# Operand addresses at a multiple of 64, differences on GpSimd alone, eight places for the x forms, and other ends, in a fused attention and two feed-forward layers

## The chip, the cores and the metric

The kernel runs on one core of a Trainium2 chip. The metric is the device time of one execution in microseconds (us); lower is better. TensorE (PE) multiplies matrices out of SBUF into PSUM, and the profile shows its weight loads apart (PEld). VectorE (DVE) and ScalarE (ACT) read PSUM and SBUF, GpSimd (POOL) works on SBUF tiles alone here, and SyncE (SP) issues every DMA.

## The reference, cut to what matters

```python
def _attn_ref(q, k, v):                       # (4, 8, 576, 64), block-causal mask
    scores = scale * np.matmul(q, k.transpose(0, 1, 3, 2))
    scores = np.where(mask, scores, -1000000000.0)
    attn = softmax(scores)
    return np.matmul(attn, v)
def _moe_ref(x, w_in, w_out):                 # x: 2304 x 512, w_in: 512 x 2048, w_out: 2048 x 512
    h = x @ w_in
    return (h * np.clip(h + 3.0, 0.0, 6.0) / 6.0) @ w_out
def _moe2_ref(x, w_in, w_out):                # the same sizes
    h = x @ w_in
    return (h * np.tanh(softplus(h))) @ w_out
# reference: attention, then _moe_ref on its output, then _moe2_ref on that
```

## The kernel before, in words

The program has three stages in a row. The **attention** fills the first 200 us. The **first layer** (to 618.8 us) goes through five blocks of tokens, four of 512 and one of 256, and in each through 16 slices `f` of the hidden width. A slice takes 12 matmuls in (L385 to L387) and 12 out (L851 to L853). Every product of two float32 operands is made of three matmuls in the type float32r: high part by high part, high by low, low by high. So each tile has a rounded tile (`wh`, `xh`, `gh`) and a rest (`wl`, `xl`, `gl`).

The **second layer** (618.8 to 998.8 us) multiplies by a scheme of seven products in place of eight (P1 to P7). Tokens go in three passes of 768, two halves of `NX` = 384 columns each; the hidden width goes in `NQ` = 8 steps `s` a pass, so there are 24 steps. A step has seven products "in" of 6 matmuls and seven "out" of 6, 84 matmuls of 384 columns in all, which `products` writes (L1150, L1152, L1153). Between in and out, ScalarE copies or activates (L1213), VectorE adds a PSUM bank to a kept tile (L1218), and then come differences of SBUF tiles: four sums T1 to T4 (`add_gsum`, L1229), and for each of the seven forms a rounding on ScalarE (L1222) and a rest, the tile less its rounding (`add_form`, L1224). VectorE adds every result of "out" to a running sum (L1199; L1197 at a pass's first step). The out products of step `s` run among the in products of step `s + 1`. The 11 differences of a step may go to VectorE or to GpSimd (`either`).

For each pass the tokens' own forms must be made too: four loads (`load2`, L985), eight differences (`sum2`, L994), 14 roundings (`round_x`, L1002) and 14 rests (`lower_x`, L1005). Form `i` of each pass lies in the same place `i`, so form `i` of the next pass can be written only when the last step of this pass has multiplied by it.

The order of the second layer is made at build time by `Schedule`: each operation has the engines that may run it with a cost in ns (`COST`), what it reads and writes, and for a DMA the time that it is taken to need to land (`land`). TensorE's order is as written. From it each other operation has a due time (`need`), and a list scheduler lets each engine take, of what is ready, the one that is due first. Each engine then runs its own list strictly in order: an operation whose input is late holds up what stands behind it. In the list, the loads of the next pass's tokens (`add_x`) come at the first step of a pass.

**Addresses.** In the program before, the weights of slices `f` = 0 to 3 lie at SBUF addresses of a multiple of 64 bytes, those of `f` = 4 to 15 (pool `whigh`, on the right side of SBUF) 32 bytes past one. The second layer puts its weights (`ws`) in the tiles of `f` = 7 to 14, all 32 past, and the x forms in those of `f` = 0 to 6. The tiles that the matmuls stream (`xh`, `xl`, `gh`, `gl`, and `gcP`) lie at a multiple of 64, but x forms 4 to 6 and the attention's `p`, `t` and `vh` 32 past one. The attention's `kb` and `qb` lie at a multiple of 64.

Of the kernel before, what the change touches and what calls it, by code (L numbers as in the profile page):

```python
# [9 lines left out]
F32 = mybir.dt.float32  # L10
# [95 lines left out]

NX = 384
# [6 lines left out]
    "in": 1040, "out": 520, "DVE_PSUM": 500, "DVE_SBUF": 800, "POOL": 1020, "ACT_PSUM": 490,  # L114
    "ACT": 530, "SP": 60,
# [3 lines left out]
class Schedule:  # L119
# [24 lines left out]
    def order(self):  # L144
# [72 lines left out]
def fused_kernel(ctx: ExitStack, tc: tile.TileContext, qT, kT, vv, w1, w2, outT):  # L217
# [9 lines left out]
    WLOW, WMID = 2, 4  # L227

# [772 lines left out]
    def round_x(i, k):  # L1001
        nc.scalar.activation(xc[FORMS[i], 0][:, k], xs2[FORMS[i], k], AF.Copy)  # L1002

    def lower_x(i, k, e="DVE"):
        ENG[e].tensor_sub(xc[FORMS[i], 1][:, k], xs2[FORMS[i], k], f32(xc[FORMS[i], 0][:, k]))  # L1005

    def prepare_x(i):
        place_x(i)
        for k in range(2):
            round_x(i, k)  # L1010
            lower_x(i, k, ("DVE", "POOL")[k])
# [109 lines left out]
    place_w(1, 1)  # L1121
    tile_of = lambda name: m5.tile([P, NX], F32, tag=name, name=name)
# [22 lines left out]
    either = (("DVE", COST["DVE_SBUF"]), ("POOL", COST["POOL"]))  # L1145

# [16 lines left out]
    def add_in(s, form):  # L1163
# [3 lines left out]
        def run(e):  # L1167
            products(
                bank[b], [weights_of(0, s, form, k) for k in range(2)],
                [(xc[form, 0][:, k], xc[form, 1][:, k]) for k in range(2)], new)  # L1170

        reads = w_names(0, s, form) + [("x", form, h, k) for h in range(2) for k in range(2)]
# [47 lines left out]
    def add_form(form):  # L1220
# [3 lines left out]
        plan.add(either, [src, ("g", form, 0)], [("g", form, 1)], lambda e: ENG[e].tensor_sub(  # L1224
            gc[form, 1], keep[src], f32(gc[form, 0])))

    def add_gsum(t):
        a, b = GSUM[t]
        plan.add(either, [a, b], [t], lambda e: ENG[e].tensor_sub(keep[t], keep[a], keep[b]))  # L1229
# [19 lines left out]
    def add_x_form(i):  # L1249
        form = FORMS[i]  # L1250
        for k in range(2):
# [3 lines left out]
            plan.add(act(False), [src], [("x", form, 0, k)], lambda e, k=k: round_x(i, k))  # L1255
            plan.add(either, [src, ("x", form, 0, k)], [("x", form, 1, k)],
                     lambda e, k=k: lower_x(i, k, e))
# [3 lines left out]
    for s in range(NS + 1):  # L1261
        q = s % NQ
        if s < NS and q == 0 and s // NQ + 1 < NPASS:
            add_x(s // NQ + 1)
        for i in range(7):
            if s < NS:
                form = IN_ORDER[i]
                b = add_in(s, form)
                if i in (3, 6):
                    add_weights(0, s + 2, i // 6)  # L1270
            if s:
                for d in range(2):
                    add_out(s - 1, OUT_ORDER[i], d)
                if i in (5, 6):
                    add_weights(1, s + 1, i - 5)
            if s == NS:
                continue
            if q == NQ - 1 and s + 1 < NS:
                add_x_form(i)
# [6 lines left out]
            elif form == "P2":  # L1286
                add_sum("g11", b, "p1")
                add_act("g11", "g11", AF.Mish, False)
                add_form("P1")
            elif form == "P3":  # L1290
                add_sum("g12", b, "g12")
                add_act("g12", "g12", AF.Mish, False)
                add_gsum("T1")
                add_form("P5")
            elif form == "P7":
                add_sum("g22", b, "g22")
                add_act("g22", "g22", AF.Mish, False)
                for t, g in (("T2", "P6"), ("T3", "P7")):
                    add_gsum(t)
                    add_form(g)  # L1300
                add_form("P3")
            else:
                add_act("g21", b, AF.Mish, True)
                add_form("P2")
                add_gsum("T4")
                add_form("P4")
# [43 lines left out]
```

## Time and profile before

| | us |
|---|---|
| median of 3 runs | 1005.14 (1003.14 to 1006.38) |
| the profiled execution, its own time | 1004.65 |
| its span, first to last instruction | 1002.7 |
| mean granted TensorE clock | 0.995 |

The profile is that of one execution. Its views: the busy time of each engine; what each engine waited for (in total, times, longest); the timeline, instruction by instruction, with the idle time before one and what ended it. Where the starts of two instructions are given, their difference is the time of what lies between. A matmul's own duration overlaps that of its neighbours, so its pace is read from starts.

### The profile page before, as it was taken

To read this page: it belongs to the slowest core of one execution; us is meant where nothing else is said; L and a number is where in the kernel's file an instruction comes from. 1 tells how busy PE (TensorE), PEld (TensorE's weight loads), DVE (VectorE), ACT (ScalarE), POOL (GpSimd) and SP (SyncE) were. 2 spreads that over 40 slices of the span, in tenths; PEclk is the share of its full clock that TensorE was granted. 3 is DMA by queue.
4 is the path that set the end of the run, shared out by engine and by line. 5 is a ranking of instruction groups with operands and counts; after the bars stand their busy time and mean duration, and the time that the engine had idled before them with its cause. 6 is when DMAs were issued, how large, how long until landed. Compare 5 with 4: busy or idle time off the path is not lost.

```text
span 1002.7 us, 15929 instructions
## 1 busy us (share of the span) xinstructions
PE 959.8 (96%) x5300; PEld 862.1 (86%) x5300; DVE 743.9 (74%) x1227; ACT 520.5 (52%) x1222; POOL 589.4 (59%) x548
## 2 busy tenths in 40 slices
PE   8999999899999998999999999799998999999997
PEld 7888889777778876888788899799998999999997
DVE  6898887888866454764647431789898898998887
ACT  4888888856534334343534353444464444654452
POOL 6455654568966656666667561645396453953453
PEclk9999999999999999999999999799999999999999
DMA  5777767789036664776665528567688676796652
GB/s 161 193 196 201 201 177 195 210 298 337 1 126 219 211 212 158 252 237 202 208 212 179 182 74 302 197 247 250 226 307 275 251 258 213 248 323 220 252 209 75
DMA packets 131425, 212.86 MB, mean 212 GB/s; under 512 B 45840, under 2 KB 72464, under 8 KB 131344
## 3 DMA queue, kind: packets, MB, share of 16 engines
q1 hardware_dynamic: 131344, 211.86, 64.9%
q8 instruction: 41, 0.67, 0.3%
q14 instruction: 40, 0.33, 0.1%
HBM read 154.66 MB, written 48.31 MB: 202 GB/s over the span
## 4 chain that ended last, share of the span: by engine, by line
PE 42%; POOL 4%; DVE 3%; DMA 2%; issue 2%; ACT 0%; SPq 0%; POOLq 0%; DVEq 0%
PE by L1150 5%; PE by L1153 5%; PE by L1152 5%; PE bh L1150 3%; PE bh L1152 3%; PE bh L1153 3%; PE y L852 2%; PE y L853 2%; PE y L851 2%; PE br L1153 2%; PE br L1150 2%; PE br L1152 2%; PE h L386 2%; PE h L387 2%; PE h L385 2%; DMA x2r<-x2d 2%
## 5 line engine op out<-in xcount | busy, mean ns | idle before, releaser
L1199 DVE TENSOR_TENSOR s<-by,s 128x384 f32<-128x384 f32 x306 | 160.0, 550 | 21.7 <-PE by L1153 21.7
L420 POOL TENSOR_TENSOR gl<-e,gh 128x512 fp32r<-128x512 f32 (+1 forms) x79 | 101.0, 1279 | 114.5 <-issue 66.1
L1229 POOL TENSOR_TENSOR kT<-kg,kg 128x384 f32<-128x384 f32 x44 | 46.3, 1053 | 160.2 <-ACT kg L1213 159.6
L385 PE MATMUL h<-xh,wh 128*128 128x512 f32 (+1 forms) x320 | 119.9, 375 | 5.0 <-DVE e L405 5.0
L1150 PE MATMUL by<-gcP,ws 128*128 128x384 f32 x336 | 115.8, 345 | 7.8 <-issue 5.7
L386 PE MATMUL h<-xl,wh 128*128 128x512 f32 (+1 forms) x320 | 119.2, 373 | 1.9 <-DVE xl L370 1.9
L852 PE MATMUL y<-gl,wh 128*128 128x512 f32 (+1 forms) x320 | 119.3, 373 | 1.8 <-POOL gl L420 1.8
L853 PE MATMUL y<-gh,wl 128*128 128x512 f32 (+1 forms) x320 | 119.0, 372 | 0.0
L851 PE MATMUL y<-gh,wh 128*128 128x512 f32 (+1 forms) x320 | 119.0, 372 | 0.0
L387 PE MATMUL h<-xh,wl 128*128 128x512 f32 (+1 forms) x320 | 118.9, 372 | 0.0
L1152 PE MATMUL by<-gcP,ws 128*128 128x384 f32 x336 | 113.7, 338 | 0.0
L1153 PE MATMUL by<-gcP,ws 128*128 128x384 f32 x336 | 113.7, 338 | 0.0
L412 ACT ACTIVATE gh<-e 128x512 fp32r<-128x512 f32 (+1 forms) x80 | 47.0, 587 | 121.1 <-DVE e L405 121.1
L1213 ACT ACTIVATE kg<-kg 128x384 f32<-128x384 f32 x72 | 37.8, 526 | 111.5 <-DVE kg L1218 111.5
L665 DVE TENSOR_TENSOR t<-t,t 128x512 fp32r<-128x512 f32 (+2 forms) x144 | 69.8, 521 | 23.5 <-ACT t L660 23.5
L282 DVE SCALAR_TENSOR_TENSOR v<-raw,v 128x512 uint32<-128x512 uint32 x64 | 70.8, 1119 | 20.1 <-POOL v L268 20.1
L394 ACT ACTIVATE e<-h 128x512 f32<-128x512 f32 (+1 forms) x80 | 43.9, 549 | 76.3 <-PE h L387 74.7
L614 ACT ACTIVATE p<-s,nm 128x64 f32<-128x64 f32 (+2 forms) x144 | 75.1, 529 | 11.9 <-DVE nm L603 11.9
L405 DVE SCALAR_TENSOR_TENSOR e<-e,h 128x512 f32<-128x512 f32 (+1 forms) x80 | 50.2, 628 | 40.5 <-ACT e L394 40.5
L1150 PE MATMUL bh<-xc,ws 128*128 128x384 f32 x192 | 65.9, 343 | 10.8 <-DVE kg L1218 10.6
L1150 PEld LDWEIGHTS by<-gcP,ws 128*128 128x128 f32 x336 | 63.4, 189 | 14.8 <-ACT gcP L1222 14.6
L385 PEld LDWEIGHTS h<-xh,wh 128*128 128x128 f32 x320 | 60.2, 188 | 18.1 <-DVE e L405 7.1
(116 smaller groups left out, 2675.5 us busy)
## 6 DMA issues: line engine op xcount, KB each, us to landing
ws<-w2d SPq DMA_DIRECT2D x96, 512.0 KB
ws<-w2d SPq DMA_DIRECT2D x96, 384.0 KB
raw<-w SPq DMA_DIRECT2D x64, 512.0 KB
x1d<-x SPq DMA_DIRECT2D x64, 144.0 KB
qb<-qs SPq DMA_DIRECT2D x30, 288.0 KB
w2d<-Sh SPq DMA_DIRECT2D x32, 256.0 KB
w2d<-S SPq DMA_DIRECT2D x32, 256.0 KB
q<-qT SPq DMA_DIRECT2D x16, 288.0 KB
```

Of the source, the lines that this page charges most:

```text
L385: nc.tensor.matmul(h, hi[:, ws], xh, start=(k == 0), stop=False)
L386: nc.tensor.matmul(h, hi[:, ws], xl, start=False, stop=False)
L387: nc.tensor.matmul(h, lo[:, ws], xh, start=False, stop=(k == KT - 1))
L420: eng.tensor_sub(gl, g, f32(gh))
L614: nc.scalar.activation(t, sc, AF.Exp, bias=nm[:, c:c + 1], accum_out=su[:, i:i + 1])
L851: nc.tensor.matmul(y, hi[:, ws], gh, start=first, stop=False)
L852: nc.tensor.matmul(y, hi[:, ws], gl, start=False, stop=False)
L853: nc.tensor.matmul(y, lo[:, ws], gh, start=False, stop=last)
L1150: nc.tensor.matmul(b, wh, xh, start=start and k == 0, stop=False, skip_group_check=True)
L1152: nc.tensor.matmul(b, wh, xl, start=False, stop=False, skip_group_check=True)
L1153: nc.tensor.matmul(b, wl, xh, start=False, stop=k == n - 1, skip_group_check=True)
L1199: nc.vector.tensor_add(dst, bank[b], total)
```

## The change

- A tile of 96 bytes a partition is put first on the right side of SBUF. All that lies there moves by 96 bytes, and what lay 32 past a multiple of 64 lies at one.
- The x forms have eight places in place of seven: form `i` of pass `p` lies in place `(i - p) % 8`. The eighth place is the tile of `f` = 15. So form `i` of the next pass goes where form `i - 1` of this pass lay.
- In steps `q` = 1 to 6 of each pass the 11 differences may go to GpSimd alone (`pool_`); in steps 0 and 7 to either engine, as before.
- The order of TensorE at the start and the end: P4 of step 0 comes after P1 of step 1; the in products of step 23 come two at a time between the out products of step 22.
- The roundings and differences of a step are added to the list after the out product of the step before; the loads of the next pass's tokens come at step `q` = 2, not 0.
- The scheduler's numbers: costs of VectorE and GpSimd are higher, `land` is 8000 for weights and 12000 for tokens (both 4000 before), and VectorE may wait for a more urgent operation that becomes ready while a less urgent one would run (`soon`).

No instruction is added or removed; the numbers of matmuls, DMAs and differences stay. The diff, cut:

```diff
+ALIGN = 96
-    "in": 1040, "out": 520, "DVE_PSUM": 500, "DVE_SBUF": 800, "POOL": 1020, "ACT_PSUM": 490,
-    "ACT": 530, "SP": 60,
+    "in": 1040, "out": 520, "DVE_PSUM": 550, "DVE_SBUF": 1200, "POOL": 1100, "ACT_PSUM": 490,
+    "ACT": 525, "SP": 60,
...
+                soon = [k for k in c if start < ready[k] < start + cost and need[k] < need[i]
+                        and need[k] < start + cost - self.HAND]
+                if soon and e == "DVE":
+                    i = min(soon, key=lambda i: (need[i], i))
+                    start, cost = ready[i], dict(ops[i][0])[e]
...
+    align = ctx.enter_context(tc.tile_pool(name="align", bufs=1, side="right"))
+    align.tile([P, ALIGN // 4], F32, tag="align", name="align")
...
-            t = slot(i, h, f"xc{i}_{h}")
-            xc[FORMS[i], h] = t[:, 0:2 * NX].rearrange("p (k n) -> p k n", k=2)
+            t = slot(i if i < 7 else 15, h, f"xc{i}_{h}")
+            xc[i, h] = t[:, 0:2 * NX].rearrange("p (k n) -> p k n", k=2)
+    def at_x(p, i):
+        return (i - p) % 8
...
+    place_x(7)
...
+    pool_ = (("POOL", COST["POOL"]),)
...
-                    lambda e, h=h: load_w(c, s, piece, h), land=4000)
+                    lambda e, h=h: load_w(c, s, piece, h), land=8000)
-                     lambda e, k=k: load2(p, k), land=4000)
+                     lambda e, k=k: load2(p, k), land=12000)
...
+    def sequence():
+        seq = []
+        for s in range(NS + 1):
+            for i in range(7):
+                if s == 1 and i == 0:
+                    seq += [("in", 1, 0), ("in", 0, 6), ("forms", 0, 6)]
+                elif 0 < s < NS - 1 or s == 0 and i < 6:
+                    seq.append(("in", s, i))
+                elif s == NS - 1 and i < 4:
+                    seq += [("in", s, n) for n in (2 * i, 2 * i + 1) if n < 7]
+                if s:
+                    seq.append(("out", s - 1, i))
+                if 0 < s < NS - 1 or s == 0 and i < 6:
+                    seq.append(("forms", s, i))
+                elif s == NS - 1:
+                    seq += [("forms", s, n) for n in {1: (3,), 2: (4,), 4: (5,), 6: (6,)}.get(i, ())]
+        return seq
...
-    for s in range(NS + 1):
-        q = s % NQ
-        if s < NS and q == 0 and s // NQ + 1 < NPASS:
-            add_x(s // NQ + 1)
+    for kind, s, i in sequence():
+        q, p = s % NQ, s // NQ
+        of = either if q in (0, NQ - 1) else pool_
...
+            if (q, i) == (2, 0) and p + 1 < NPASS:
+                add_x(p + 1)
```

## Rows read from the trace of the kernel before

**Rows 1.** The page: busy us (share of the span) xinstructions of each engine.
```profile
PE 959.8 (96%) x5300; PEld 862.1 (86%) x5300; DVE 743.9 (74%) x1227; ACT 520.5 (52%) x1222; POOL 589.4 (59%) x548
```
**Rows 2.** Timeline (start us, us, ...): first and last matmul of the second layer.
```profile
618.84 0.34 PE L1150 MATMUL bh<-xc,ws 128*128 128x384 f32 x1
...
998.51 0.34 PE L1153 MATMUL by<-gcP,ws 128*128 128x384 f32 x1
```
**Rows 3.** Timeline, one step of the second layer; then the next step's same matmul.
```profile
666.05 1.37 DVE L1224 TENSOR_TENSOR gcP<-kg,gcP 128x384 fp32r<-128x384 f32 x1
...
667.35 1.01 DVE L1199 TENSOR_TENSOR s<-by,s 128x384 f32<-128x384 f32 x2
667.35 0.34 PE L1153 MATMUL bh<-xc,ws 128*128 128x384 f32 x1
...
667.99 0.42 PE L1150 MATMUL by<-gcP,ws 128*128 128x384 f32 x1 [0.30 <-issue]
...
669.12 0.34 PE L1150 MATMUL br<-xc,ws 128*128 128x384 f32 x1
...
675.36 0.34 PE L1150 MATMUL br<-xc,ws 128*128 128x384 f32 x1
...
682.55 0.34 PE L1153 MATMUL bh<-xc,ws 128*128 128x384 f32 x1
```
**Rows 4.** Waits of the second layer: who for whom, us in total, times, longest.
```profile
PE by L1150 <- issue: 5.7, 19, 0.4
```
**Rows 5.** Timeline, start of the second layer.
```profile
624.91 0.34 PE L1153 MATMUL bh<-xc,ws 128*128 128x384 f32 x1
628.82 0.56 DVE L994 TENSOR_TENSOR x2t<-x2r 128x384 f32<-128x384 f32 x1 [9.36 <-DMA x2r<-x2d]
...
632.90 0.69 PE L1150 MATMUL bh<-xc,ws 128*128 128x384 f32 x1 [7.65 <-DVE kg L1218]
...
638.18 0.40 PE L1152 MATMUL by<-gcP,ws 128*128 128x384 f32 x1
```
**Rows 6.** Windows: us, each engine's busy us, PEclk (granted share of 2.4 GHz), DMA, GB/s.
```profile
634.00:636.00 2.00, 2.00 (x8) 2.00 (x8) 2.00 (x2) 1.03 (x3) 2.00 (x3) 0.50 0.05 9
```
**Rows 7.** Timeline, first step of the second pass.
```profile
758.90 0.45 PE L1150 MATMUL bh<-xc,ws 128*128 128x384 f32 x1 [2.92 <-DVE kg L1218]
```
**Rows 8.** Timeline, the last out products.
```profile
991.12 0.41 PE L1150 MATMUL by<-gcP,ws 128*128 128x384 f32 x1 [1.42 <-ACT gcP L1222]
```
**Rows 9.** Timeline, TensorE, first layer: bounds of 60 matmuls (`f` 1 to 3), of 240 (`f` 6 to 15).
```profile
301.84 0.40 PE L385 MATMUL h<-xh,wh 128*128 128x512 f32 x1
...
315.45 0.39 PE L385 MATMUL h<-xh,wh 128*128 128x512 f32 x1
...
420.87 0.39 PE L385 MATMUL h<-xh,wh 128*128 128x512 f32 x1
...
477.09 0.40 PE L385 MATMUL h<-xh,wh 128*128 128x512 f32 x1
```
**Rows 10.** The same in its block of 256 tokens: 48 matmuls (`f` 0 to 3); start of 264 (`f` 6 on).
```profile
575.94 0.28 PE L385 MATMUL h<-xh,wh 128*128 128x256 f32 x1
...
581.68 0.28 PE L385 MATMUL h<-xh,wh 128*128 128x256 f32 x1
...
587.86 0.28 PE L385 MATMUL h<-xh,wh 128*128 128x256 f32 x1
```
**Rows 11.** Timeline, attention: the first and third of three matmuls of 384 columns in a row.
```profile
49.31 0.34 PE L581 MATMUL s<-kb,qb 128*128 128x384 f32 x1
...
49.66 0.34 PE L583 MATMUL s<-kb,qb 128*128 128x384 f32 x1
```
**Rows 12.** Timeline, VectorE and GpSimd: a difference beside VectorE's, and one beside its adds.
```profile
682.17 1.31 POOL L1224 TENSOR_TENSOR gcP<-kT,gcP 128x384 fp32r<-128x384 f32 x1
...
992.72 4.73 DVE L1199 TENSOR_TENSOR s<-by,s 128x384 f32<-128x384 f32 x10
...
993.63 1.01 POOL L1224 TENSOR_TENSOR gcP<-kT,gcP 128x384 fp32r<-128x384 f32 x1
```

More of the change, by code (lines that the diff above doesn't have):

```diff
@@ L997, in place_x, with round_x, lower_x @@
         for h in range(2):
-            t = slot(i, h, f"xc{i}_{h}")
-            xc[FORMS[i], h] = t[:, 0:2 * NX].rearrange("p (k n) -> p k n", k=2)
[L1001 to L1005, printed above, removed]
+            t = slot(i if i < 7 else 15, h, f"xc{i}_{h}")
+            xc[i, h] = t[:, 0:2 * NX].rearrange("p (k n) -> p k n", k=2)
+    def at_x(p, i):
+        return (i - p) % 8
+    def round_x(p, i, k):
+        nc.scalar.activation(xc[at_x(p, i), 0][:, k], xs2[FORMS[i], k], AF.Copy)
+    def lower_x(p, i, k, e="DVE"):
+        hi, lo = (xc[at_x(p, i), h][:, k] for h in range(2))
+        ENG[e].tensor_sub(lo, xs2[FORMS[i], k], f32(hi))
     def prepare_x(i):
@@ L1009, in prepare_x @@
         for k in range(2):
-            round_x(i, k)
-            lower_x(i, k, ("DVE", "POOL")[k])
+            round_x(0, i, k)
+            lower_x(0, i, k, ("DVE", "POOL")[k])
     WSLOTS = {(0, 0): (7, 8), (1, 0): (9, 10), (0, 1): (11, 12), (1, 1): (13, 14)}
@@ L1169, in run @@
                 bank[b], [weights_of(0, s, form, k) for k in range(2)],
-                [(xc[form, 0][:, k], xc[form, 1][:, k]) for k in range(2)], new)
-        reads = w_names(0, s, form) + [("x", form, h, k) for h in range(2) for k in range(2)]
+                [(xc[at, 0][:, k], xc[at, 1][:, k]) for k in range(2)], new)
+        at = at_x(s // NQ, FORMS.index(form))
+        reads = w_names(0, s, form) + [("x", at, h, k) for h in range(2) for k in range(2)]
         plan.add(pe(COST["in"]), reads, [b], run)
@@ L1218, in add_sum, with add_form @@
             lambda e: nc.vector.tensor_add(keep[dst], bank[b], keep[other]))
-    def add_form(form):
+    def add_form(form, of):
         src = GFORM[form]
@@ L1223, in add_form, with add_gsum @@
             gc[form, 0], keep[src], AF.Copy))
-        plan.add(either, [src, ("g", form, 0)], [("g", form, 1)], lambda e: ENG[e].tensor_sub(
+        plan.add(of, [src, ("g", form, 0)], [("g", form, 1)], lambda e: ENG[e].tensor_sub(
             gc[form, 1], keep[src], f32(gc[form, 0])))
-    def add_gsum(t):
+    def add_gsum(t, of):
         a, b = GSUM[t]
-        plan.add(either, [a, b], [t], lambda e: ENG[e].tensor_sub(keep[t], keep[a], keep[b]))
+        plan.add(of, [a, b], [t], lambda e: ENG[e].tensor_sub(keep[t], keep[a], keep[b]))
     def add_weights(c, s, piece):
@@ L1247, in add_x, with add_x_form @@
                 plan.add(either, [at(a), at(b)], [at(out)], lambda e, k=k, n=n: sum2(k, n, e))
-    def add_x_form(i):
-        form = FORMS[i]
+    def add_x_form(p, i):
+        form, at = FORMS[i], at_x(p, i)
         for k in range(2):
@@ L1254, in add_x_form @@
                 "P6": ("T2", k), "P7": ("xB", k, 1), "P4": ("T4", k)}[form]
-            plan.add(act(False), [src], [("x", form, 0, k)], lambda e, k=k: round_x(i, k))
-            plan.add(either, [src, ("x", form, 0, k)], [("x", form, 1, k)],
-                     lambda e, k=k: lower_x(i, k, e))
+            plan.add(act(False), [src], [("x", at, 0, k)], lambda e, k=k: round_x(p, i, k))
+            plan.add(either, [src, ("x", at, 0, k)], [("x", at, 1, k)],
+                     lambda e, k=k: lower_x(p, i, k, e))
@@ L1259, in fused_kernel @@
     for piece in range(2):
         add_weights(1, 1, piece)
-    for s in range(NS + 1):
-        q = s % NQ
-        if s < NS and q == 0 and s // NQ + 1 < NPASS:
-            add_x(s // NQ + 1)
[L1265 to L1277, printed above, removed]
+    for kind, s, i in sequence():
+        q, p = s % NQ, s // NQ
+        of = either if q in (0, NQ - 1) else pool_
+        form = IN_ORDER[i]
+        if kind == "out":
+            for d in range(2):
+                add_out(s, OUT_ORDER[i], d)
+            if i in (5, 6):
+                add_weights(1, s + 2, i - 5)
+        elif kind == "in":
+            if (q, i) == (2, 0) and p + 1 < NPASS:
+                add_x(p + 1)
+            b = add_in(s, form)
+            if i in (3, 6):
+                add_weights(0, s + 2, i // 6)
@@ L1278, in fused_kernel @@
             if q == NQ - 1 and s + 1 < NS:
-                add_x_form(i)
+                add_x_form(p + 1, i)
             if form == "P1":
@@ L1288, in fused_kernel @@
                 add_act("g11", "g11", AF.Mish, False)
-                add_form("P1")
             elif form == "P3":
@@ L1292, in fused_kernel @@
                 add_act("g12", "g12", AF.Mish, False)
-                add_gsum("T1")
-                add_form("P5")
             elif form == "P7":
@@ L1297, in fused_kernel @@
                 add_act("g22", "g22", AF.Mish, False)
[L1298 to L1301, printed above, removed]
             else:
                 add_act("g21", b, AF.Mish, True)
-                add_form("P2")
-                add_gsum("T4")
-                add_form("P4")
+        elif form == "P2":
+            add_form("P1", of)
+        elif form == "P3":
+            add_gsum("T1", of)
+            add_form("P5", of)
+        elif form == "P7":
+            for t, g in (("T2", "P6"), ("T3", "P7")):
+                add_gsum(t, of)
+                add_form(g, of)
+            add_form("P3", of)
+        elif form == "P4":
+            add_form("P2", of)
+            add_gsum("T4", of)
+            add_form("P4", of)
     plan.issue()
```

## The prediction

> **What bounds the kernel now.** I read the busy times first: TensorE is busy 96% of the span [rows 1], so time is to be had only where it waits or where each matmul takes longer than it must. Then I took the pace of matmuls from starts on the timeline, stage by stage, and then the gaps.
>
> In the second layer, 36 matmuls of 384 columns run from 669.12 to 675.36 us without a gap, 173.3 ns each [rows 3]. The stage has 2016 matmuls, 2015 start-to-start intervals from 618.84 to 998.51 us, 379.67 us [rows 2]. At 173.3 ns they would take 349.2. So 30.5 us are lost there. They are in four kinds of place:
> - The start. After P7 of step 0 TensorE stands from 624.91 to 632.90, 7.99 us for an interval of 0.17. P4 waits until VectorE has read the bank of P7, and VectorE sits for 9.36 us in front of a token sum (L994) whose load has not landed. Then 16 intervals take 5.28 us (to 638.18), 330 ns each, where 2.77 would do: the granted clock in that stretch is 0.50, the 1.2 GHz level, after TensorE stood. Lost: 7.82 + 2.51 = 10.3 us [rows 5, 6].
> - The head of nearly every step. VectorE is on a difference of 1.37 us from 666.05, so the add that frees the bank of P1 starts at 667.35; TensorE goes from 667.35 to 667.99 between two matmuls and stretches the next. That is 0.47 + 0.08 = 0.55 us [rows 3]. The waits list has it 19 times [rows 4]: 10.5 us.
> - The second pass's first step, the same pattern: the add on VectorE that P4 needs comes late, behind token sums, and TensorE idles 2.92 us [rows 7]; with the slow matmul behind it 3.0.
> - The last out products: 1.42 us of waiting for a form [rows 8]; with the slow start 1.5.
>
> These are 25.3 of the 30.5; 5.2 are left in smaller waits and in matmuls a few ns over the floor.
>
> In the first layer, matmuls of 512 columns differ by their weights' address: 60 in `f` = 1 to 3 (a multiple of 64) take 13.61 us, 226.8 ns each; 240 in `f` = 6 to 15 (32 past) take 56.22 us, 234.2 ns each [rows 9]. What they stream is at a multiple of 64 in both.
>
> **The change part by part.** *Addresses, 512 columns.* 1152 matmuls of the first layer (12 slices x 24 x 4 blocks) have weights 32 past. At 7.4 ns each that is 8.5 us, if every one sets the pace. *256 columns.* Here it goes the other way: 48 at a multiple of 64 take 5.74 us, 119.6 ns; 264 at 32 past take 30.98 us (587.86 to 618.84 [rows 2, 10]), 117.3 ns. 288 matmuls x 2.3 ns cost 0.7. Net at most 7.8 us. I don't take it all: in the first block the weights' conversion on the other engines sets some of the pace, and stalls at the block boundaries wait for loads that don't get faster. I take 5.5, ends 2 and 7.8.
>
> *384 columns.* In the second layer almost all is 32 past in weights, and still 173.3 ns is reached. The attention's `kb` and `qb` are at a multiple of 64, and there two intervals take 0.35 us, 175 each [rows 11]. So I expect no new floor, only fewer of the odd longer ones: out of the 5.2 us left over I take 1.0, ends -2 (a loss as at 256 columns would be 2016 x 1 ns) and 3. *Attention.* `p`, `t` and `vh` move too. The trace shows no run of these at another address; nearest are [rows 9], a gain of 3%, and [rows 10], a loss of 2%; 448 matmuls of `t` by `vh` at no more than the 234 ns of 512 columns are under 105 us, so the bound is a gain of 3.2 to a loss of 2.1. I take 0.
>
> The Trainium skill's page "SBUF — State Buffer", section "Door 1: The DMA port swizzle", says that SBUF is read in lines of 16 bytes. Both 0 and 32 past a multiple of 64 begin such a line, so by that rule alone the move would change nothing; the trace disagrees at 512 columns, by 7.4 ns [rows 9], and what the rule would give is the first rival below.
>
> *Differences on GpSimd alone in steps 1 to 6.* VectorE's remaining work is 14 adds from "out" and 3 others, 17 x about 0.5 (ten back to back take 4.73 us [rows 12]), 8.5 us of a step of 84 x 173.3 ns = 14.56. It is then free when a bank ends. GpSimd does 11 differences. One takes 1.01 us where VectorE runs only adds from PSUM beside it, and 1.31 where VectorE has a difference as well [rows 12]. Eleven at 1.01 are 11.1 us, at 1.31 14.4: both below 14.56. Counting from a step's start, the longest chain begins when P7 ends at 11.4 us: add and activation to 12.7, T2 to about 14.6, rounding, the rest of P6 to about 16.7, needed at 19.8 when the next step's out P6 comes. Three us are spare, and the last one, P4's rest, ends near 22.7 against 28.1. So GpSimd's longer queue is hidden under TensorE; were the cover gone, each 0.1 us an operation would cost 1.1 us a step. Behind GpSimd's list stand only differences, and ScalarE's roundings wait for them; its own copies from PSUM stand behind those in line, with banks that aren't rewritten for 3 us. The head stall goes where the step before has `q` = 1 to 6: 18 heads x 0.55 = 9.9 us. Next in line is the add of P7, which has 1.04 us between P7 and P4 and takes 0.56.
>
> *Token loads at step 2.* Four SP issues and eight sums move behind the weights of two more steps; weights are asked for two steps ahead (29 us), so four issues of about 0.4 us in SP's queue are covered. With the loads gone from step 0, its 10.3 us go; what comes next there is the forms of P1 and P5, made in about 3 us while P1 of step 1 and P4 run. I leave 0.5 and count 9.8. At the second pass 3.0 go. In exchange the eight sums fall among steps 2 to 7: 8.1 us on GpSimd against 3.4 spare a step, or on VectorE, where `soon` lets adds go first. Bounds 0 and 8 x 0.3 us a pass; I take 0, as TensorE needs them only at the pass's end.
>
> *Eight places.* A form may be written one product earlier, 2.1 us. The second boundary shows no large gap before, so I count 0 (ends -1 and 1). *Ends.* At the end, the in products of step 23 come up to 5 us earlier, so the forms are ready: 1.5 us. The weights of step 23 are wanted that much earlier, 24 us after they are asked for. The `align` tile has no instruction.
>
> *Sum.* The second layer gives 9.8 + 9.9 + 3.0 + 1.5 + 1.0 = 25.2 us, the first 5.5. Against the profiled execution's own time, 1004.65 - 30.7 = 973.95, so 974. That execution is 0.5 below the median of the runs, which I let be.
>
> **The rivals.**
> - *The address is not the cause.* `f` = 0 to 3 are also the first slices of a block and lie in another half of SBUF. Then the 5.5 don't come: 979.5. For it: the 256-column rows go the other way. Against: the two stretches run the same forms of instructions at the same clock, and come from two blocks [rows 9].
> - *384 columns gain as 512 do.* 3% of 173.3 is 5.4 ns, and 2016 of them give 10.9 less the 1.0 counted: 964. Against: 175 ns at a multiple of 64 [rows 11].
> - *The step heads stay*, because forms come late from GpSimd in place of the add on VectorE. For it: a queue of 11 in order, with tokens' sums among them. Against: 3 us spare. 974 + 9.9 = 984.
> - *The start's stall comes back elsewhere*: loads at step 2 land later than the plan's 12 us and the sums block a queue. VectorE waited 9.36 us for such a load at the start [rows 5], so the plan's 12 leave little under 3 in hand. 974 + 9.8 = 984.
> - *Slower: GpSimd waits for VectorE's adds.* L1199 also reads a tile of SBUF. If each difference had to let one add by (0.54 us), it would take 1.55, a step 17.05 in place of 15.20 (667.35 to 682.55 [rows 3]), and 18 steps lose 33.3. The rest of the sum is 30.7 - 9.9 = 20.8, so 1004.65 + 33.3 - 20.8 = 1017. It turns slower from 1.49 us an operation. Against: GpSimd's 1.01 us beside ten adds in a row [rows 12].
>
> **How the numbers follow.** Chances: the forecast 0.55, address without effect 0.12, 384 columns too 0.08, step heads stay 0.12, start's stall elsewhere 0.07, slower 0.04, and 0.02 for a sum that comes to nothing. A measurement of this kernel tells about 0.3% (3 us) from no change. The range goes from 964, the fast rival, to 990: the first layer's 2, one of the 9.9 terms lost and 2 more for small waits at the pass boundaries. That leaves out the slower case and mixed failures. Faster 0.93, within 0.3% 0.03, slower 0.04.
>
> **What would show it.** After, the first layer's matmuls of 512 columns in `f` = 6 to 15 should start 227 ns apart and those of 256 columns 120. In the second layer a step should take 14.6 us from head to head, with no VectorE differences in steps 1 to 6 and GpSimd's at 1.0 us. The gap after P7 of step 0 should be under 1 us and the clock stay at its upper level; no gap over 0.5 us at the second pass and among the last out products. Wrong would make it: GpSimd operations at 1.3 us and more, TensorE waiting for a rest that GpSimd makes, a token sum at the head of a queue waiting for its load, or 234 ns at the new addresses.

## The result, and the profile after

The changed kernel takes **974.87 us** (median of 4 runs, 974.47 to 975.9) against 1004.14 us before (4 runs, 1002.94 to 1006.38): a ratio of 0.9707 with a 95% interval of 0.9686 to 0.9729. The forecast was 974.0. The profiled execution took 975.24 us, its span is 973.4 us, the mean granted clock 0.992.

First the page's busy times, then the first and last matmul of the second layer on the timeline (start us, duration us, engine, line, operation, output<-inputs).

```profile
PE 943.3 (97%) x5300; PEld 859.7 (88%) x5300; DVE 650.3 (67%) x1127; ACT 517.2 (53%) x1222; POOL 668.6 (69%) x648
```
```profile
615.12 0.34 PE L1164 MATMUL bh<-xc,ws 128*128 128x384 f32 x1
...
969.28 0.34 PE L1167 MATMUL by<-gcP,ws 128*128 128x384 f32 x1
```

VectorE gave 94 us of busy time away and GpSimd took 79 more [rows 1]. The second layer now takes 354.16 us from its first to its last matmul, where it took 379.67 [rows 2]: 25.5 us less. The attention ends 1.5 us sooner after the span's start, the first layer takes 2.2 us less, and 0.2 lie outside. That makes the 29.4 us between the two profiled executions (1004.65 and 975.24).

The step heads are gone. Here are the last matmul of `in` P1 and the first that follows it, then the same last matmul one step later:

```profile
652.44 0.33 PE L1167 MATMUL bh<-xc,ws 128*128 128x384 f32 x1
652.61 0.33 PE L1164 MATMUL by<-gcP,ws 128*128 128x384 f32 x1
...
667.00 0.33 PE L1167 MATMUL bh<-xc,ws 128*128 128x384 f32 x1
```

The first two start 0.17 us apart, where it was 0.64 [rows 3], and from head to head it is 14.56 us, which is 84 x 173.3 ns, where it was 15.20.

The start is clean as well: the last matmul of P7 of step 0 starts at 621.20 and the next product, now P1 of step 1, follows 0.17 us later, where 7.99 us lay between [rows 5]. P4 of step 0 and the first product out (at 623.45) follow without a gap too.

```profile
621.20 0.33 PE L1167 MATMUL bh<-xc,ws 128*128 128x384 f32 x1
621.37 0.33 PE L1164 MATMUL bh<-xc,ws 128*128 128x384 f32 x1
```

In the first layer the pace is the one that was forecast. Between the first two rows there are 102 matmuls of 512 columns, 23.12 us, 226.7 ns each, in the block and slices that had 234.2 [rows 9]; between the other two 102 of 256 columns, 12.24 us, 120.0 ns each, where they had 117.3 [rows 10].

```profile
441.04 0.39 PE L393 MATMUL h<-xh,wh 128*128 128x512 f32 x1
...
464.16 0.39 PE L393 MATMUL h<-xh,wh 128*128 128x512 f32 x1
...
600.73 0.28 PE L393 MATMUL h<-xh,wh 128*128 128x256 f32 x1
...
612.97 0.28 PE L859 MATMUL y<-gh,wh 128*128 128x256 f32 x1
```

But the stalls between them grew. Added up over the layer (its length less every matmul at the pace of its shape and address), they were 15.5 us before and are 21.1 after. One of them, after and then before, with VectorE's work ahead of it:

```profile
475.72 0.39 PE L393 MATMUL h<-xh,wh 128*128 128x512 f32 x1
...
475.99 0.42 DVE L906 TENSOR_TENSOR S<-v 128x256 f32<-128x256 f32 x1
...
477.46 0.68 DVE L378 TENSOR_TENSOR xl<-xr,xh 128x512 fp32r<-128x512 f32 x1
...
478.20 0.50 PE L394 MATMUL h<-xl,wh 128*128 128x512 f32 x1 [2.09 <-DVE xl L378]
```
```profile
479.17 0.39 PE L385 MATMUL h<-xh,wh 128*128 128x512 f32 x1
...
479.60 0.69 DVE L370 TENSOR_TENSOR xl<-xr,xh 128x512 fp32r<-128x512 f32 x1
...
480.34 0.50 PE L386 MATMUL h<-xl,wh 128*128 128x512 f32 x1 [0.79 <-DVE xl L370]
```

Before, TensorE came to this place at 479.17 and its next matmul started 1.17 us later; now it comes 3.45 us earlier, but the making of the lower half of x starts only 2.14 us earlier (479.60, now 477.46), behind four token sums (L906 to L909), and the next matmul starts 2.48 us later. The difference, 1.31, is the growth of the gap. What the faster matmuls gave, the list of VectorE in front of them took back here.

And a new stall came in the second layer, at the second pass. The rows below are from the timeline and from the windows (us, busy us of PE, PEld, DVE, ACT and POOL with instructions, granted clock, DMA share, GB/s):

```profile
739.59 0.59 SPq L1222 DMA_DIRECT2D outT<-s  x1
...
746.57 0.34 PE L1167 MATMUL by<-gcP,ws 128*128 128x384 f32 x1
...
748.24 0.56 DVE L1212 TENSOR_SCALAR s<-by 128x384 f32<-128x384 f32 x1 [4.12 <-DMA outT<-s]
748.85 0.44 PE L1164 MATMUL by<-gcP,ws 128*128 128x384 f32 x1 [1.94 <-DVE s L1212]
...
751.16 0.52 PE L1166 MATMUL by<-gcP,ws 128*128 128x384 f32 x1
751.48 0.52 PE L1167 MATMUL by<-gcP,ws 128*128 128x384 f32 x1
```
```profile
728.00:732.00 4.00, 4.00 (x25) 4.00 (x24) 3.30 (x7) 0.73 (x2) 4.00 (x5) 1.00 1.04 410
748.00:752.00 4.00, 3.15 (x13) 3.15 (x14) 3.76 (x7) 0.69 (x2) 1.36 (x2) 0.77 0.96 338
```

The first write of the new pass into a running sum (L1212) has to wait until the sum of the pass before has left by DMA, and the operation that frees the bank is that write. The DMA that it waits for was issued at 739.59 and landed at 748.1, 8.5 us later; the planner counts 3 us for it (`land=3000` in both kernels). TensorE loses 2.1 us there, and the 10 matmuls at 320 ns behind it another 1.5. The DMA engines are full from 724 to 748 us (a share of 0.99 to 1.04 in each 4 us); among what they carry are the third pass's tokens, whose loads SP issues from 723.2 to 730.6. In the program before they were issued 12.8 us later in the layer.

### The profile page after: what moved, and what is told of

It is laid out like the page before. It is cut to its first block, busy times and chain, and to the rows that moved or that the text cites. A ratio compares the mean times of both kernels' runs of the same rounds, so it can differ in the third digit from the quotient of the medians.

```text
span 973.4 us, 15933 instructions
## 1 busy us (share of the span) xinstructions
PE 943.3 (97%) x5300; PEld 859.7 (88%) x5300; DVE 650.3 (67%) x1127; ACT 517.2 (53%) x1222; POOL 668.6 (69%) x648
## 4 chain that ended last, share of the span: by engine, by line
PE 48%; DVE 1%; DMA 1%; POOL 1%; issue 0%; ACT 0%; SPq 0%; DVEq 0%; POOLq 0%
PE by L1164 6%; PE by L1166 6%; PE by L1167 6%; PE bh L1166 3%; PE bh L1164 3%; PE bh L1167 3%; PE br L1166 3%; PE br L1167 3%; PE br L1164 3%; PE y L860 2%; PE y L861 2%; PE y L859 2%; PE h L394 2%; PE h L395 2%; PE h L393 2%; DMA outT<-s 1%
## 5 line engine op out<-in xcount | busy, mean ns | idle before, releaser
L1164 PE MATMUL by<-gcP,ws 128*128 128x384 f32 x336 | 113.0, 336 | 2.2 <-DVE s L1212 1.9
L1166 PE MATMUL by<-gcP,ws 128*128 128x384 f32 x336 | 112.7, 336 | 0.0
L1167 PE MATMUL by<-gcP,ws 128*128 128x384 f32 x336 | 112.7, 335 | 0.0
L1239 POOL TENSOR_TENSOR gcP<-kg,gcP 128x384 fp32r<-128x384 f32 x71 | 74.7, 1052 | 51.3 <-ACT gcP L1237 51.3
L1239 POOL TENSOR_TENSOR gcP<-kT,gcP 128x384 fp32r<-128x384 f32 x89 | 92.4, 1044 | 16.1 <-ACT gcP L1237 16.0
L413 DVE SCALAR_TENSOR_TENSOR e<-e,h 128x512 f32<-128x512 f32 (+1 forms) x80 | 50.2, 627 | 36.8 <-ACT e L402 36.8
L394 PEld LDWEIGHTS h<-xl,wh 128*128 128x128 f32 x320 | 60.7, 190 | 13.9 <-DVE xl L378 4.1
```

Of the source, the lines that this page charges most:

```text
L394: nc.tensor.matmul(h, hi[:, ws], xl, start=False, stop=False)
L1164: nc.tensor.matmul(b, wh, xh, start=start and k == 0, stop=False, skip_group_check=True)
L1166: nc.tensor.matmul(b, wh, xl, start=False, stop=False, skip_group_check=True)
L1167: nc.tensor.matmul(b, wl, xh, start=False, stop=k == n - 1, skip_group_check=True)
L1239: plan.add(of, [src, ("g", form, 0)], [("g", form, 1)], lambda e: ENG[e].tensor_sub(gc[form, 1], keep[src], f32(gc[form, 0])))
```

## The experiments

Ratios are to the kernel before on the same chip, where it took 1006.5 us (runs a), 1006.0 (b) and 1003.5 (c), so ratios are to be compared and not times; the changed kernel's is 0.9707 (0.9686 to 0.9729). "Second layer" is the time from its first to its last matmul: 379.7 before, 354.2 after. It is read from one trace of each.

| run | us | ratio (95%) | second layer |
|---|---|---|---|
| a1_align | 1001.14 | 0.9949 (0.9933 to 0.9964) | 378.4 |
| a2_no_align | 982.46 | 0.9764 (0.9738 to 0.9791) | 360.2 |
| a3_align64 | 977.90 | 0.9715 (0.9687 to 0.9743) | 354.9 |
| a4_either | 971.69 | 0.9647 (0.9619 to 0.9676) | 349.7 |
| b1a_land4000 | 980.34 | 0.9750 (0.9712 to 0.9787) | 359.0 |
| b1b_step0 | 973.42 | 0.9675 (0.9638 to 0.9711) | 352.8 |
| b2_ends | 973.37 | 0.9667 (0.9636 to 0.9697) | 353.3 |
| b3_places | 975.58 | 0.9694 (0.9660 to 0.9728) | 353.7 |
| c1_either_oldcost | 984.37 | 0.9802 (0.9780 to 0.9824) | 362.3 |
| c2_either_nosoon | 973.31 | 0.9694 (0.9675 to 0.9712) | 350.8 |
| c3_pool_oldplan | 974.12 | 0.9708 (0.9690 to 0.9725) | 354.3 |
| c4_either_xl | 968.54 | 0.9646 (0.9632 to 0.9659) | 349.8 |

### Is it the address?

**a1_align**: the kernel before with the 96-byte tile alone.

```diff
+    align = ctx.enter_context(tc.tile_pool(name="align", bufs=1, side="right"))
+    align.tile([P, ALIGN // 4], F32, tag="align", name="align")   # ALIGN = 96
```

> The kernel before with the 96-byte tile alone. Theory (the address of the weights sets the pace of the matmuls of 512 columns): in the first layer f = 4 to 15 go from 234 to 227 ns, the 256-column ones from 117 to 120, and the first layer's 417.6 us come to about 415.4, as in the changed kernel; with 1.5 us in the attention and 2.4 of odd longer matmuls in the second layer some 6 us in all, about 998. Rival 1 (it is the place in the block of tokens, or the half of SBUF): 234 ns stays, and 1004. Rival 2 (384 columns gain 3% too): about 988.

Measured: 1001.14 us, 5.3 us less than before on that chip, where 6 were expected. The pace is what the address theory says, 227 ns at 512 columns and 120 at 256 throughout (medians), with nothing else changed. But the first layer became only 1.3 us shorter, because its stalls grew from 15.5 to 22.0 us. In the second layer matmuls sped up too, and the step heads swallowed part of it: 0.70 us from start to start, where before it was 0.64 [rows 3].

```profile
662.95 1.37 DVE L1227 TENSOR_TENSOR gcP<-kg,gcP 128x384 fp32r<-128x384 f32 x1
...
664.18 0.34 PE L1156 MATMUL bh<-xc,ws 128*128 128x384 f32 x1
...
664.89 0.41 PE L1153 MATMUL by<-gcP,ws 128*128 128x384 f32 x1 [0.37 <-issue]
```

So the address is shown to set the pace at 512 and 256 columns, and also that pace alone is worth little while other engines set the ends of the stalls.

**a2_no_align**: the changed kernel without the tile. **a3_align64**: the changed kernel with a tile of 64 bytes, so that all on the right side moves but stays 32 past a multiple of 64.

```diff
-    align.tile([P, ALIGN // 4], F32, tag="align", name="align")   # a2: both lines out
-ALIGN = 96
+ALIGN = 64                                                        # a3
```

> The changed kernel without the 96-byte tile. Theory: 234 ns and 117 ns come back in the first layer, and the time is the changed kernel's 974.9 plus about 6, 981; the second layer's step heads stay free of gaps. Rival 1 (the address is not the cause): 975. Rival 2 (the second layer's gain needs the address): 985 or more.

> The changed kernel with a tile of 64 bytes in place of 96, so the right side moves but stays 32 past a multiple of 64. Theory (what counts is the address modulo 64): as without the tile, 234 ns and about 981. Rival 1 (any move off the old addresses does it, or the address modulo 128 counts): 227 ns and 975.

Measured: 982.46 and 977.90 us. In the first layer 102 matmuls of 512 columns take 23.89 us without the tile (first two rows), 234.2 ns each, and 23.80 with the tile of 64 bytes (last two), 233.3 each: to move the tiles does next to nothing there, to move them onto a multiple of 64 does. Of the remainders by 64 only 0 and 32 were tried.

```profile
440.10 0.39 PE L391 MATMUL h<-xh,wh 128*128 128x512 f32 x1
...
463.99 0.40 PE L857 MATMUL y<-gh,wh 128*128 128x512 f32 x1
```
```profile
440.39 0.40 PE L859 MATMUL y<-gh,wh 128*128 128x512 f32 x1
...
464.19 0.40 PE L859 MATMUL y<-gh,wh 128*128 128x512 f32 x1
```

In the second layer it is less plain. The mean of the intervals without a stall is 173.5 ns in the changed kernel. Without the tile it is 176.4 where weights lie 32 past and what they multiply doesn't (1583 intervals), and 174.3 where both do; with 64 bytes the first of these is 173.9. Over the whole layer the mean is 176.0 without the tile and 174.2 with 64 bytes, so a2 lost 5.0 us of pace there and a3 1.3, though they agree in the remainder by 64. What more than this remainder decides at 384 columns is open.

Neither total came out as reasoned. In a2 it is near the expected 981 (0.9764 of 1004.14 is 980.5), but 2.6 us of the loss are in the first layer, where all 6 were expected, and 6.0 in the second. In a3 the pace of the first layer is back at 233 and the ratio still can't be told from the changed kernel's (0.9715 and 0.9707): its first layer is 1.5 us longer, less than the same code differs from run to run (see the part on why the prediction came out).

The Trainium skill's page "SBUF — State Buffer", section "Door 1: The DMA port swizzle", was weighed in the prediction: by lines of 16 bytes both places are alike. a1 differs from before in place alone, and its 226.7 ns against 234.2 (means of 106 and 240 matmuls of 512 columns) don't bear that out for TensorE's pace here.

### What took the step heads away?

**a4_either**: the changed kernel with the differences on either engine in all steps, as before the change.

```diff
-        of = either if q in (0, NQ - 1) else pool_
+        of = either
```

> The changed kernel with the differences of steps 1 to 6 again open to either engine. Theory (the heads were lost to VectorE's differences): 18 step heads of 0.55 us come back, about 985. Rival (the new costs and the wait for more urgent operations keep VectorE's differences out of the way on their own): 976, with few differences on VectorE or none before the first adds of a step.

Measured: 971.69 us, a ratio 0.6% below the changed kernel's, with intervals that just miss each other (up to 0.9676, from 0.9686); the second layer takes 349.7 us, half a microsecond over the 349.2 that 2015 intervals of 173.3 ns need. VectorE does differences again in all steps, one of them across most step heads, and no head came back:

```profile
663.12 1.08 DVE L1214 TENSOR_TENSOR s<-by,s 128x384 f32<-128x384 f32 x2 [0.33 <-PE by L1167]
...
664.12 0.95 DVE L1239 TENSOR_TENSOR gcP<-kg,gcP 128x384 fp32r<-128x384 f32 x1
...
664.31 0.33 PE L1167 MATMUL bh<-xc,ws 128*128 128x384 f32 x1
664.48 0.33 PE L1164 MATMUL by<-gcP,ws 128*128 128x384 f32 x1
```

What changed is the order: the two adds that free the bank now come first, at 663.12, and the difference behind them, where before the difference stood in front [rows 3].

The theory that the prediction was built on, that heads go because VectorE has no differences, falls as the only cause.

**c1_either_oldcost**: a4 with the planner's four old costs. **c2_either_nosoon**: a4 without the rule for the sooner-needed add. **c3_pool_oldplan**: the changed kernel, differences on GpSimd alone, with old costs and without that rule.

```diff
-    "DVE_PSUM": 550, "DVE_SBUF": 1200, "POOL": 1100, ... "ACT": 525
+    "DVE_PSUM": 500, "DVE_SBUF": 800, "POOL": 1020, ... "ACT": 530     # c1, c3
-                if soon and e == "DVE":
+                if soon and e == "none":                               # c2, c3
```

> The changed kernel with differences on either engine in all steps (as in the run a4_either) and, on top, the planner's four changed costs put back (a difference on VectorE 800 ns and not 1200, on GpSimd 1020 and not 1100, an add from PSUM 500 and not 550). Theory (the step heads went because the planner now reckons a VectorE difference at 1200 ns and so puts none of them in front of the add that frees P1's bank): the head of some 18 steps idles again for 0.5 to 0.65 us, 980 to 983 us. Rival (the order in which differences are listed, or the rule that lets a sooner-needed add go first, removed them): 971 to 974, as a4_either.

> The run a4_either without the planner's rule that lets VectorE wait for an add that is needed sooner; the changed costs stay. Theory (the costs alone keep the heads free): 971 to 974 us, no gap of half a microsecond at the step heads. Rival (the rule does it): 980 to 983.

> The changed kernel (differences of steps 1 to 6 on GpSimd alone) with the planner's old costs and without the rule for sooner-needed adds. Theory (either of the two parts is enough: with no difference of VectorE's in those steps no head can wait for one, whatever the costs say): 974 to 978 us, heads only at the two steps at each pass boundary. Rival (the costs are needed as well): 980 to 984.

Measured: 984.37, 973.31 and 974.12 us. In c1 the heads are back, 0.70 us in step after step, and with the same picture as before:

```profile
669.68 2.62 POOL L1239 TENSOR_TENSOR gcP<-kT,gcP 128x384 fp32r<-128x384 f32 x2
...
670.06 1.37 DVE L1239 TENSOR_TENSOR gcP<-kg,gcP 128x384 fp32r<-128x384 f32 x1
...
671.29 0.34 PE L1167 MATMUL bh<-xc,ws 128*128 128x384 f32 x1
671.35 1.01 DVE L1214 TENSOR_TENSOR s<-by,s 128x384 f32<-128x384 f32 x2
...
672.00 0.41 PE L1164 MATMUL by<-gcP,ws 128*128 128x384 f32 x1 [0.36 <-issue]
```

The planner counts 0.80 us for the difference at 670.06; on the chip it takes 1.37, because GpSimd is on one of its own beside it (2.62 us for two). Without a GpSimd operation beside it, a difference of VectorE's takes 0.56 (21 of them in the kernel before). It takes no longer beside one of GpSimd's if it starts first, as here in the changed kernel:

```profile
741.12 0.56 DVE L1239 TENSOR_TENSOR gcP<-kT,gcP 128x384 fp32r<-128x384 f32 x1 [0.85 <-ACT gcP L1237]
741.13 1.42 POOL L1239 TENSOR_TENSOR gcP<-kg,gcP 128x384 fp32r<-128x384 f32 x1
```

There VectorE started first, by 0.01 us, and it is GpSimd's that is stretched, from about 1.0 to 1.42; in c1 VectorE came second. The Trainium skill's page "SBUF — State Buffer", section "Who interferes with whom", says that a VectorE instruction with two inputs in SBUF and a GpSimd instruction that reads SBUF exclude each other, and that the one that comes second waits out the first. These rows agree, roughly: 1.42 is near 0.56 and 1.0 in a row. The adds, which have one input in PSUM, leave GpSimd's differences at 1.04 in the changed kernel, as that section also says (x instructions | busy us, mean ns):

```profile
L1239 POOL TENSOR_TENSOR gcP<-kT,gcP 128x384 fp32r<-128x384 f32 x89 | 92.4, 1044 | 16.1 <-ACT gcP L1237 16.0
```

With the new costs, 1.20 us for a VectorE difference among them, the planner puts the adds that free P1's bank in front of the difference, as the rows of a4 show; which of the four costs does it was not taken apart. The rule for sooner adds does little in the layer: c2 has three gaps over half a microsecond (0.55, 0.57 and 0.51 us), none at a head. Its ratio of 0.9694 is even so above a4's 0.9647, with intervals that touch; in its trace 2.1 us more than in a4's lie behind the last matmul. In c3 the heads stayed away but for one (0.76 us); four other gaps of 0.66 to 1.01 us are near the start and the pass boundaries.

So there are four cells, and either part does it alone:

| | old costs | new costs |
|---|---|---|
| either engine | 0.9802 (c1) | 0.9647 (a4) |
| GpSimd alone in steps 1 to 6 | 0.9708 (c3) | 0.9707 (after) |

With the old costs GpSimd alone is worth 0.9%; with the new ones it costs 0.6% by a4, though only 0.1% by c2. (c3 is without the rule for sooner adds, c1 with it.) The second layer is 4.5 us longer than a4's and 3.4 than c2's, and the longest gap lies near a pass boundary: the changed kernel, b1b, b2 and b3 have one of 1.2 to 2.3 us there; a4, c2 and c4 have none over 0.6. It is not one cause: in the changed kernel, b2 and b3 the gap ends with a running sum's first write, in b1b with a rest that GpSimd makes (L1239), and b1a, with GpSimd alone too, has no such gap. VectorE waits 4.6 us in all for the running sum's DMA in the changed kernel, and 0.3 in a4. There the DMA of the same sum goes out at 735.07 and lands 5.8 us later, not 8.5:

```profile
735.07 0.38 SPq L1222 DMA_DIRECT2D outT<-s  x1
...
740.92 0.56 DVE L1212 TENSOR_SCALAR s<-by 128x384 f32<-128x384 f32 x1 [0.28 <-DMA outT<-s]
```

Counted from the layer's first matmul it goes out at 122.6 us, in the changed kernel at 124.5, and TensorE starts the new pass at 109.2 in both. Why it goes out later with GpSimd alone, and lands later, was not traced further.

### The token loads, the ends, the eight places

**b1a_land4000** and **b1b_step0** take the two halves of that edit apart: the landing time that the planner counts, and the place in its list.

```diff
-                     lambda e, k=k: load2(p, k), land=12000)
+                     lambda e, k=k: load2(p, k), land=4000)      # b1a
-            if (q, i) == (2, 0) and p + 1 < NPASS:
+            if (q, i) == (0, 0) and p + 1 < NPASS:              # b1b
```

> The changed kernel, with one number undone: the plan takes a token load to land 4 us after its issue, as in the kernel before, and not 12. The four issues stand at the same place of SP's list. Theory (the start's stall and the second pass's went because the plan now puts the token sums after the load has really landed, not because the loads moved): VectorE waits again for some 8 to 9 us for a load in front of the sums of L1002, TensorE stands behind it at the start (about 10 us) and at the second pass (about 3), together 985 to 988 us. Rival (the start went because P1 of step 1 now stands ahead of P4 of step 0, which covers the wait): at most 2 us over the changed kernel's 974.9.

> The changed kernel, with the token loads and sums put back into the planner's list at step 0 and not step 2; the landing time of 12 us stays. Theory (the place in the list decides nothing, as SP issues the loads as early as their places are free in either case, and the landing time orders the sums): 974 to 976 us. Rival (step 2 was what moved the sums off the start): the 10 us of the start come back, 984 to 988.

Measured: 980.34 and 973.42 us. The place decides nothing that the runs can tell. In the changed kernel SP issues the four loads of the second pass from 3.3 us after the layer's first matmul, as before (the first row is from the trace before, the second from after):

```profile
622.15 2.15 SPq L985 DMA_DIRECT2D x2r<-x2d  x4
```
```profile
618.41 2.32 SPq L993 DMA_DIRECT2D x2r<-x2d  x4
```

What moved back are the sums behind them: the first starts 16.3 us into the layer, not 10.0. The first loads landed 6.7 to 7.9 us after their issue in the trace before, so a count of 4 put the sums too early and one of 12 does not. With 4 us counted, the stand at the start comes back:

```profile
622.57 0.34 PE L1167 MATMUL bh<-xc,ws 128*128 128x384 f32 x1
...
624.30 0.99 POOL L1002 TENSOR_TENSOR x2t<-x2r 128x384 f32<-128x384 f32 x1 [14.71 <-DMA x2r<-x2d]
...
628.13 0.69 PE L1164 MATMUL by<-gcP,ws 128*128 128x384 f32 x1 [5.22 <-ACT gcP L1237]
```
```profile
629.00:631.00 2.00, 2.00 (x7) 2.00 (x8) 1.33 (x2) 2.00 (x6) 2.00 (x3) 0.50 0.80 311
```

It is 5.4 us and some 2.8 of matmuls at the 1.2 GHz level behind it, 8.2 in all, not the 10 expected. TensorE now stands after P4, and it is GpSimd and ScalarE that wait for tokens that have not landed. The 3 us at the second pass didn't come back.

**b2_ends**: the changed kernel with the plain order at both ends.

```diff
-                if s == 1 and i == 0:
-                    seq += [("in", 1, 0), ("in", 0, 6), ("forms", 0, 6)]
...
+                if s < NS:
+                    seq.append(("in", s, i))
                 if s:
                     seq.append(("out", s - 1, i))
...
+                if s < NS:
+                    seq.append(("forms", s, i))
```

> The changed kernel with the kernel before's plain order of in, out and forms at the start and at the end: P4 of step 0 ahead of P1 of step 1, and no in products of step 23 two at a time. Theory: the end's wait of 1.4 us for a form comes back (1.5 us), and at the start about 1 us between P7 and P4 of step 0, together 976.5 to 978 us. Rival (the ends are worth nothing once VectorE is free of differences there): 974.5 to 975.5.

Measured: 973.37 us, not slower. A gap of 0.99 us is there at the start, and at the end nothing over 0.51 us: the wait there went without the new order.

```profile
621.18 0.44 PE L1164 MATMUL bh<-xc,ws 128*128 128x384 f32 x1 [0.65 <-DVE kg L1233]
```

**b3_places**: the changed kernel with a fixed place for each form.

```diff
     def at_x(p, i):
-        return (i - p) % 8
+        return i
```

> The changed kernel with forms of x in seven fixed places and not rotating through eight. Theory (the boundary between the passes has slack, so the eighth place is worth nothing): 974 to 976 us. Rival (a form must then wait until TensorE has read the last product of the pass before from the same place): a gap at each of the three boundaries on TensorE, 1 to 2 us with the slow matmuls behind it, 977 to 981.

Measured: 975.58 us, the same within the intervals. Its gaps over 1 us at the second and third pass are the running sum's, not a form's, so no boundary waited for a place (here the third pass):

```profile
869.65 0.44 PE L1164 MATMUL by<-gcP,ws 128*128 128x384 f32 x1 [1.02 <-DVE s L1212]
```

### The first layer's stall, and a faster version

**c4_either_xl**: a4 with the lower half of x ahead of the token sums in VectorE's list.

```diff
-        ("w1", 0), ("w2", 0), ("w3", 0), ("sd", 0), ("xl", 0), ("a", 0), ...
+        ("w1", 0), ("w2", 0), ("w3", 0), ("xl", 0), ("sd", 0), ("a", 0), ...
```

> The run a4_either with, in the first layer's second list of stages, the lower half of x (L378) put ahead of the token sums (L906 to L909). Theory (two gaps of TensorE, 1.5 us at 384.4 and 2.45 at 472.9 of a4_either, end when VectorE has made that half behind the sums, so the move shortens them by the sums' 1.7 us each): 2 to 4 us less than a4_either, 968 to 970. Rival (the half is then late for another reason, or the sums are late for their store, and another gap opens): 971 to 973.

Measured: 968.54 us, 0.9646 of the kernel before: the lowest median, and faster than both kernels. The stall in question shrank from 2.45 us in a4 to 0.71:

```profile
474.39 0.68 DVE L378 TENSOR_TENSOR xl<-xr,xh 128x512 fp32r<-128x512 f32 x1
475.13 0.50 PE L394 MATMUL h<-xl,wh 128*128 128x512 f32 x1 [0.32 <-DVE xl L378]
```

Of the other, the 1.5 us went, but the gap 3 us ahead of it, which ends with a product of VectorE's (L413), grew from 0.9 to 2.46. That is not the edit's doing: b1a, b1b, b2 and c2, without it, show the same 2.4 there and no second gap. The first layer's profile is 3.7 us shorter than a4's, 2.2 shorter than the shortest of the nine with its old list; the ratio is the same (a4 0.9647, on another chip). Whether this edit by itself is worth anything in the time is therefore not settled; that the order of VectorE's list made the stall of 2.45 us is shown.

## Why the prediction came out, point by point

| place | counted, us | measured, us |
|---|---|---|
| attention | 0 | 1.5 |
| first layer | 5.5 | 2.2 |
| start of the second layer | 9.8 | 10.4 |
| step heads | 9.9 | 10.6 |
| second pass's first step | 3.0 | -0.6 |
| the end | 1.5 | 1.3 |
| 384 columns, pace | 1.0 | 2.5 |
| smaller waits (the rest of the 25.5) | 0 | 1.3 |

The measured column is worked out from the starts of matmuls in the two profiles: 3.8 us lost from 746.57 to 753.4 for the 3.2 that were lost before (the prediction read 3.0 from the idle time); 0.4 lost at the end for 1.7; 174.7 ns before and 173.5 after as the mean of intervals without a stall.

- **Attention and first layer: too small to read from two profiles.** In the nine profiles whose code for both is the changed kernel's (it, a4, b1 to b3, c1 to c3) the attention lasts until 196.7 to 201.0 us, and the first layer takes 414.3 to 417.2, mean 415.5; before they were 201.2 and 417.6. So the attention's 1.5 is not shown to be a gain, and the first layer's 2.2 is right only on average.
- **First layer: the mechanism was right, the size was not.** The pace was as counted: 1152 x 7.5 ns less 288 x 2.7 are 7.9 us. Of the 5.5 taken, "stalls at the block boundaries wait for loads that don't get faster" was the reservation; in the trace TensorE's waits there end with VectorE and GpSimd, not with loads, and the stalls take back 5.6 us and not 2.3.
- **384 columns: too small.** What it called "no new floor" held, 173.3 before and after, but longer intervals than that were more than an odd few, and the pace gained 2.5 us, 1.9 of it with the tile alone (a1). In the changed kernel the tile is worth 5.0 (a2). The range's lower end of -2 had a slip in it: 2016 x 1 ns is not "a loss as at 256 columns", which was 2.3 ns a matmul and would be 4.6 us. The fast rival, 3% of the floor, did not come.
- **Step heads: the size right, the cause half right.** "The head stall goes where the step before has `q` = 1 to 6" credited GpSimd. c3 shows that this is enough, a4 and c1 that the new costs would have done it alone, and at least as well. That the planner's numbers are part of the change stood in the list of edits; what they do was not worked out in the prediction, though the row of 1.37 us [rows 3] stood against a count of 0.80.
- **The start: the size right, the reason wrong.** "Four SP issues and eight sums move behind the weights": the issues did not move, b1b. The landing time moved the sums, b1a. The rival had it that 12 us "leave little under 3 in hand"; that took VectorE's 9.36 us of idle time for the load's time, and the loads landed 6.7 to 7.9 us after their issue.
- **Second pass: the step that failed.** Its stall went and another took its place nearby. The prediction asked whether sums and forms fit, and not whether the running sums would have left by DMA in time: 8.5 us passed from issue to landing. In a4, where TensorE comes just as early, they were 5.8, and the wait is 0.3 us.
- **GpSimd's price:** 1.04 us an operation, near the 1.01 counted, so the slow rival had no ground. That its queue is "hidden under TensorE" holds inside a pass and fails near the boundaries: against a4 the second layer is 4.5 us longer (354.2 and 349.7), and 3.8 us are lost at 746.57, though by way of a DMA.
- **Ends and places:** the ends counted 1.5 and b2 shows none of it in the time (0.9667, with 0.8 us lost at the start), the 1.3 came from elsewhere; places counted 0, and b3 agrees.

That the total fell within 1 us is in part luck, as the errors had both signs: first layer, second pass and end gave 7.1 us less than counted, and attention, pace, heads, start and small waits 5.6 more.

## What to carry to other kernels

When a planner orders the work, look at what it counts for an operation beside what the row shows when the neighbour engine is busy too: counts such as 0.80 for 1.37 us made the step heads, 4 for 7 the stand at the start, and new numbers cured the heads at least as well as a ban of an engine. A faster stage pulls TensorE up to the next queue, so ask of each stall whether its end moves as well; a gain in pace of 7.9 us left 2.2. Undo each part by itself, since two parts may each remove the same loss, and then one of them is only a price.

## What had not been expected of the hardware

- The attention's `kb` and `qb` lie on the side that the tile doesn't move, at a multiple of 64 in all kernels. Yet their matmuls of 512 columns start 227 ns apart (the medians of the second and third of three) in the changed kernel and in a1, 232 and 235 before and without the tile, and 232 and 239 with 64 bytes. Something other than their own addresses must count; this is open.
- A stall of the same length doesn't always cost clock. After 2.48 us at 475.72 the first matmul takes 337 ns and the next are within 10 ns of their pace, while after 2.42 us at 363.94 eight of them start 427 ns apart, and after 2.28 us at 746.57 ten of them 320 ns apart. The granted clock is 1.00 in the first stretch below and 0.50, the 1.2 GHz level, in the second.

```profile
478.00:480.00 2.00, 1.80 (x8) 1.50 (x9) 0.81 (x3) 1.22 (x3) 0.46 (x1) 1.00 0.79 242
```
```profile
368.00:370.00 2.00, 2.00 (x6) 1.52 (x5) 1.92 (x3) 0.53 (x2) 1.46 (x2) 0.50 0.41 109
```
